# The four tiles of split weights put at four different places within 128 bytes of SBUF

## The chip, the cores and the metric

The kernel runs on one core of a Trainium2 chip. The metric is the device time of one launch in microseconds (us). The kernel before was timed in three runs: median 892.65 us, lowest 891.91, highest 894.43.

## The reference

Three parts follow each other. First an attention over 4 batches, 8 heads, 576 positions and 64 dimensions, mixed with a read of a memory matrix. Then two layers of experts over the 2304 rows of 512 numbers that the attention gives. Each layer picks one of 8 experts for a row and runs that expert's two products.

```python
local = np.matmul(softmax(mask(q @ k.T / 8)), v)
attn  = g * mem_out + (1 - g) * local        # -> x, 2304 rows of 512
# layer 1, layer 2 (same shape, other weights, other routing):
idx   = argmax(logits, axis=1)
for e in range(8):
    mask = idx == e
    h = np.maximum(x[mask] @ w1[e], 0.0)      # 512 -> 1024
    out[mask] = gate_w[mask, None] * (h @ w2[e])   # 1024 -> 512
```

## The kernel before, in words

The attention takes about the first 290 us. After it come two layers of steps. Each step takes 128 rows that go to one expert, gathers them, multiplies by `w1` (512 by 1024), applies the ReLU, multiplies by `w2` (1024 by 512) and writes 128 rows out.

The products are made in a 4-byte format (`F32R`) of less than full precision. To keep the precision, both operands are split into a high part and a low remainder, and each product is three matmuls: high rows by high weights, high rows by low weights, low rows by high weights (`mms`, L1235). One step has 48 such matmuls of 512 columns: 24 for `w1` (into `ph0` and `ph1`) and 24 for `w2` (into `py`). The rows are the stationary operand (128 by 128), the weights are the moving operand (512 columns, 2,048 bytes of each partition).

The split weights lie in four tiles. `Wh0` and `Wl0` are the high and low parts of `w1`, `Wh1` and `Wl1` those of `w2`. So in the trace `ph<-Wh` reads `Wh0`, `ph<-Wl` reads `Wl0`, `py<-Wh` reads `Wh1` and `py<-Wl` reads `Wl1`. Each tile has two halves of 16 KB of each partition: PE reads one half (`self.pv`) while the next expert's weights are split into the other (`self.wv`). Which half it is comes from a register, so the address of a matmul's weights is made by register instructions on PE's queue ahead of it. The order listings call them REGISTER_ALU (one operation) and ISA (several operations in one instruction); the trace calls them ALU_OP and FUSED_REGOPS.

A split of one eighth of an expert's weights (a chunk, 128 by 1024) is two instructions: ACT copies the staged chunk from `stg` to the high tile (`split_hi`, L898), DVE subtracts that from the staged chunk and writes the low tile (`split_lo`, L901). The chunks come in by DMAs that SP issues (`dma_chunks`).

The four tiles are taken one behind the other from a pool (`wp`, L1156 to L1158). In the built program of before they begin at bytes 69,344, 102,112, 134,880 and 167,648 of each partition. Each of these is 96 more than a multiple of 128, and since every matmul begins a multiple of 2,048 bytes into a half, every matmul's weights begin at 96 within 128 bytes too. The split rows (`b`, the stationary operand) also begin at 96; the rows of the second layer's first step (`x0`) begin at 32.

## Time and profile before

| what | us |
|---|---|
| median of three runs | 892.65 |
| lowest, highest | 891.91, 894.43 |
| the profiled execution, its own time | 894.2 |
| its span, first to last instruction | 892.4 |
| PE busy (matmuls) | 858.1 |
| DVE busy | 507.8 |
| ACT busy | 474.4 |

The profiled execution's time is 1.8 us more than its span. Matmuls are pipelined and the trace models their ends, so that one matmul's record reaches over the start of the next; what a matmul costs in a dense row of them is read from the distance between starts, not from its duration.

### The profile page before, as it was taken

To read this page: it belongs to the slowest core of one execution; us is meant where nothing else is said; L and a number is where in the kernel's file an instruction comes from. 1 tells how busy PE (TensorE), PEld (TensorE's weight loads), DVE (VectorE), ACT (ScalarE), POOL (GpSimd) and SP (SyncE) were. 2 spreads that over 40 slices of the span, in tenths; PEclk is the share of its full clock that TensorE was granted. 3 is DMA by queue.
4 is the path that set the end of the run, shared out by engine and by line. 5 is a ranking of instruction groups with operands and counts; after the bars stand their busy time and mean duration, and the time that the engine had idled before them with its cause. 6 is when DMAs were issued, how large, how long until landed. Compare 5 with 4: busy or idle time off the path is not lost. (4 is left out here: it accounts for less than half of the span.)

```text
span 892.4 us, 20618 instructions
## 1 busy us (share of the span) xinstructions
PE 858.1 (96%) x5187; PEld 675.0 (76%) x5187; DVE 507.8 (57%) x1589; ACT 474.4 (53%) x940; POOL 276.4 (31%) x375
## 2 busy tenths in 40 slices
PE   5999999999999999999999999999989999999996
PEld 2777677777668777877888877877868888888885
DVE  5657567568575866387536676644466414463520
ACT  3657657667566635376545545432366425564531
POOL 5457636536531111221221221211132112321221
PEclk9999999999999999999999999999999999999998
DMA  8424453423215266188424317022688415384111
GB/s 131 82 44 95 79 169 94 83 45 84 55 23 204 71 225 214 49 270 274 145 79 127 106 47 228 27 51 56 220 264 276 139 48 156 128 303 131 44 38 40
DMA packets 139813, 110.30 MB, mean 124 GB/s; under 512 B 107258, under 2 KB 107258, under 8 KB 139652
## 3 DMA queue, kind: packets, MB, share of 16 engines
q1 hardware_dynamic: 129252, 85.03, 33.3%
q0 software_dynamic: 8032, 23.22, 7.9%
q8 instruction: 53, 0.87, 0.4%
q14 instruction: 108, 0.88, 0.3%
q10 hardware_dynamic: 2368, 0.30, 0.2%
HBM read 90.32 MB, written 19.25 MB: 123 GB/s over the span
## 5 line engine op out<-in xcount | busy, mean ns | idle before, releaser
L1235 PE MATMUL py<-Wh,b 128*128 (+1 forms) x688 | 240.7, 406 | 2.5 <-DVE b L1179 2.4
L1235 PE MATMUL ph<-Wh,b 128*128 (+1 forms) x672 | 227.9, 400 | 0.7 <-ACTq L1246 0.7
L901 DVE TENSOR_TENSOR Wl<-stg,Wh 128x1024 f32 (+1 forms) x120 | 145.4, 1224 | 81.7 <-ACT Wh L898 71.7
L1235 PEld LDWEIGHTS py<-Wh,b 128*128 128x128 f32 x688 | 129.3, 188 | 32.5 <-issue 4.7
L1235 PEld LDWEIGHTS ph<-Wh,b 128*128 128x128 f32 x672 | 126.8, 189 | 27.1 <-ACTq L1246 1.1
L898 ACT ACTIVATE Wh<-stg 128x1024 f32 (+1 forms) x120 | 125.6, 1058 | 25.9 <-DVEq L1246 7.5
L1235 PE MATMUL py<-Wl,b 128*128 (+1 forms) x344 | 134.8, 392 | 0.0
L1235 PE MATMUL ph<-Wl,b 128*128 (+1 forms) x336 | 131.9, 392 | 2.1 <-DVEq L1246 2.0
L1179 DVE TENSOR_TENSOR b<-pt,b 128x512 fp32r<-128x512 f32 x86 | 59.4, 691 | 104.1 <-ACT b L1178 103.2
L263 ACT ACTIVATE att<-psat 128x512 f32<-128x512 f32 (+1 forms) x144 | 66.6, 463 | 78.2 <-PE psat L261 77.4
L284 PE MATMUL psav<-vb,att 128*128 128x128 f32 (+1 forms) x640 | 97.6, 283 | 0.9 <-ACT att L263 0.8
L284 PEld LDWEIGHTS psav<-vb,att 128*128 128x128 f32 x640 | 81.7, 192 | 20.9 <-ACT att L263 9.9
L1342 POOL DMA_INDIRECT out_dram<-ysb,xca x21 | 26.9, 1282 | 192.4 <-ACTq L1246 122.9
L1178 ACT ACTIVATE b<-pt 128x512 fp32r<-128x512 f32 x86 | 51.5, 598 | 62.9 <-PE pt L1347 61.7
L244 ACT ACTIVATE a<-a,mx 128x128 f32<-128x128 f32 (+3 forms) x128 | 71.0, 555 | 9.6 <-DVE mx L209 9.6
L1235 PEld LDWEIGHTS ph<-Wl,b 128*128 128x128 f32 x336 | 63.7, 190 | 14.8 <-DVEq L1246 2.7
L1235 PEld LDWEIGHTS py<-Wl,b 128*128 128x128 f32 x344 | 64.9, 189 | 9.8
L1337 ACT ACTIVATE ysb<-py,xca 128x512 f32<-128x512 f32 x42 | 28.8, 686 | 76.1 <-PE py L1235 65.4
L1144 POOL DMA_INDIRECT xg<-x_scratch,idx x48 | 55.9, 1165 | 40.5 <-POOL xca L1331 11.2
L209 DVE CUSTOM_DVE_ANT_0 a<-pss,wmask 128x128 f32<-128x128 f32 (+3 forms) x128 | 60.6, 478 | 9.0 <-PE pss L231 6.7
L1459 POOL DMA_DIRECT2D x_scratch<-xcb x21 | 11.9, 566 | 163.4 <-DVEq L1246 61.6
L261 PE MATMUL psat<-ident,a 128*128 128x128 f32 x320 | 58.2, 280 | 0.7 <-ACT a L244 0.6
(376 smaller groups left out, 1246.5 us busy)
## 6 DMA issues: line engine op xcount, KB each, us to landing
stg<-in_moe_w_dram SPq DMA_DIRECT2D x120, 512.0 KB, 4.9
x_scratch<-ysb POOLq DMA_DIRECT2D x22, 256.0 KB, 2.8
qkn<-in_q_dram SPq DMA_DIRECT2D x64, 72.0 KB, 2.5
qkn<-in_k_dram SPq DMA_DIRECT2D x60, 72.0 KB, 2.4
vb<-in_v_dram SPq DMA_DIRECT2D x32, 128.0 KB, 2.3
x_scratch<-xb SPq DMA_DIRECT2D x16, 256.0 KB, 3.3
x_scratch<-stg SPq DMA_DIRECT2D x11, 258.0 KB, 3.8
xg<-x_scratch,idx POOLq DMA_INDIRECT x48, 4.1
```

Of the source, the lines that this page charges most:

```text
L209: nc.vector.tensor_tensor_reduce(out=out, in0=ps, in1=mask, scale=-0.125, scalar=bound, op0=ALU.add, op1=ALU.min, accum_out=m)
L244: nc.scalar.activation(out=a[:, 0:N], in_=a[:, 0:N], func=AF.Exp, scale=-1.0, bias=mx, accum_out=rs_t[pi][:, c, j:j + 1])
L261: nc.tensor.transpose(ps[:, 128 * i:128 * i + 128], x, ident)
L263: nc.scalar.activation(out=att[:, 0:N], in_=ps[:, 0:N], func=AF.Copy)
L284: nc.tensor.matmul(av_t[pi][:, c, j:], att[:, 128 * kb:128 * kb + 128], vn[:, kb, j:, 0:D], start=(kb == 0), stop=(kb == c))
L898: return nc.scalar.activation(out=chunk(Wh, c, wv), in_=stg[:, c].unsqueeze(1), func=AF.Copy).ins
L901: return nc.vector.tensor_tensor(out=chunk(Wl, c, wv), in0=stg[:, c].unsqueeze(1), in1=chunk(Wh, c, wv).bitcast(F32), op=ALU.subtract).ins
L1144: return nc.gpsimd.indirect_dma_start(out=rows_of(t), out_offset=None, in_=rows, in_offset=bass.IndirectOffsetOnAxis(ap=idx[:, L, t:t + 1] ...
L1178: nc.scalar.activation(out=hi, in_=ps, func=AF.Copy)
L1179: nc.vector.tensor_tensor(out=lo, in0=ps, in1=hi.bitcast(F32), op=ALU.subtract)
L1235: mm = nc.tensor.matmul(ps, x[:, col:col + P], W, start=(first and q_ == qs[0]), stop=(last and q_ == qs[-1]))
L1337: nc.scalar.activation(out=ysb, in_=py, func=AF.Copy, scale=xc[:, 0:1])
```

## The change

The four tiles are still taken from the same pool in the same order. `Wh1` is made 4 elements (16 bytes) longer and used from its fifth element on, `Wl1` 16 elements (64 bytes) longer and used from its seventeenth on. The pool rounds the size of the longer `Wh1` up, so that `Wl0` and `Wl1` begin 32 bytes later as well.

```diff
     wp = ctx.enter_context(tc.tile_pool(name="wp", bufs=1, reuse_waits="tile"))
-    Wh.extend(wp.tile([P, 2, 4096], F32R, name=f"Wh{i}") for i in range(2))
-    Wl.extend(wp.tile([P, 2, 4096], F32R, name=f"Wl{i}") for i in range(2))
+    wt = lambda nm, o: wp.tile([P, 8192 + o], F32R, name=nm)[:, o:].rearrange("p (v n) -> p v n", v=2)
+    Wh.extend((wt("Wh0", 0), wt("Wh1", 4)))
+    Wl.extend((wt("Wl0", 0), wt("Wl1", 16)))
```

| tile | first byte used before | after | within 128: before | after |
|---|---|---|---|---|
| `Wh0` | 69,344 | 69,344 | 96 | 96 |
| `Wh1` | 102,112 | 102,128 | 96 | 112 |
| `Wl0` | 134,880 | 134,912 | 96 | 0 |
| `Wl1` | 167,648 | 167,744 | 96 | 64 |

No other tile moves. The number of instructions that compute or move data, their order on each engine and every semaphore wait are the same in both programs. What differs is how addresses are made. PE in one step of the first layer, at the start of the second product, before:

```order
L1235 ISA
L1235 MATMUL py<-Wh_3930,b_4031 128x512
L1235 REGISTER_ALU
L1235 MATMUL py<-Wl_3932,b_4031 128x512
L1235 MATMUL py<-Wh_3930,b_4032 128x512
L1347 MATMUL pt_3940<-ident,hs_4025 128x128 x4
```

The same place after (all lines behind the change stand one lower in the file):

```order
L1236 ISA
L1236 MATMUL py<-Wh_3930,b_4031 128x512
L1236 ISA
L1236 MATMUL py<-Wl_3932,b_4031 128x512
L1236 MATMUL py<-Wh_3930,b_4032 128x512
L1348 MATMUL pt_3940<-ident,hs_4025 128x128 x4
```

The one-operation instruction that made the address of `Wl1` from that of `Wh1` has become one with several operations. This is so at 160 places of the program, all of them on `Wl1`. DVE at the split of the first chunk of `w2`, before:

```order
L1246 COMPARE_AND_BRANCH
L901 ISA
L901 TENSOR_TENSOR Wl_3932<-stg,Wh_3930 128x1024
L1246 UNCONDITIONAL_BRANCH x2
L1262 UNCONDITIONAL_BRANCH
```

and after:

```order
L1247 COMPARE_AND_BRANCH
L901 ISA x2
L901 TENSOR_TENSOR Wl_3932<-stg,Wh_3930 128x1024
L1247 UNCONDITIONAL_BRANCH x2
L1263 UNCONDITIONAL_BRANCH
```

One more register instruction stands ahead of the split. This is so at 50 places; DVE's program has 757 of these instructions at this line in place of 707.

## Rows read from the trace of the kernel before

**Rows 1.** The page: busy time of the engines, TensorE's granted clock by slices.
```profile
PE 858.1 (96%) x5187; PEld 675.0 (76%) x5187; DVE 507.8 (57%) x1589; ACT 474.4 (53%) x940; POOL 276.4 (31%) x375
PEclk9999999999999999999999999999999999999998
```

**Rows 2.** The page's costliest groups: busy us, mean ns | idle before, releaser.
```profile
L1235 PE MATMUL py<-Wh,b 128*128 (+1 forms) x688 | 240.7, 406 | 2.5 <-DVE b L1179 2.4
L1235 PE MATMUL ph<-Wh,b 128*128 (+1 forms) x672 | 227.9, 400 | 0.7 <-ACTq L1246 0.7
...
L1235 PE MATMUL py<-Wl,b 128*128 (+1 forms) x344 | 134.8, 392 | 0.0
L1235 PE MATMUL ph<-Wl,b 128*128 (+1 forms) x336 | 131.9, 392 | 2.1 <-DVEq L1246 2.0 <-DVE Wl L901 0.2
```

**Rows 3.** The timeline, 502.0 to 505.5 us: start, duration, instruction.
```profile
502.03 0.39 PE L1235 MATMUL ph<-Wl,b 128*128 x1
...
502.26 0.62 PE L1235 MATMUL ph<-Wh,b 128*128 x2
...
502.65 2.15 ACT L898 ACTIVATE Wh<-stg 128x1024 f32 x2
502.71 0.39 PE L1235 MATMUL ph<-Wl,b 128*128 x1
...
503.73 2.54 DVE L901 TENSOR_TENSOR Wl<-stg,Wh 128x1024 f32 x2 [2.19 <-ACT Wh L898]
...
505.43 0.39 PE L1235 MATMUL ph<-Wl,b 128*128 x1
```

**Rows 4.** Windows: length, busy of PE, PEld, DVE, ACT, POOL, granted clock, DMA, GB/s.
```profile
501.81:505.43 3.62, 3.62 (x17) 3.00 (x16) 1.61 (x2) 3.32 (x5) 2.09 (x5) 1.00 0.16 57
600.60:603.20 2.60, 0.06 (x3) 0.00 (x0) 1.15 (x9) 0.69 (x1) 0.72 (x3) 1.00 0.03 7
604.20:606.90 2.70, 2.29 (x5) 1.72 (x6) 0.23 (x1) 0.00 (x0) 0.00 (x0) 0.50 0.30 100
300.00:892.40 592.40, 573.76 (x3037) 465.75 (x3036) 311.50 (x838) 284.50 (x420) 124.24 (x177) 0.99 0.43 139
```

**Rows 5.** The timeline of PE, 605 to 607 us.
```profile
605.20 1.05 PE L1235 MATMUL ph<-Wh,x 128*128 x2
606.05 0.63 PE L1235 MATMUL ph<-Wl,x 128*128 x1
606.48 0.63 PE L1235 MATMUL ph<-Wh,x 128*128 x1
606.91 0.41 PE L1288 MATMUL pm<-ident,ysb 128*128 128x128 f32 x1
```

**Rows 6.** The timeline of PE, 612.5 to 612.9 us.
```profile
612.54 0.39 PE L1235 MATMUL ph<-Wl,x 128*128 x1
612.76 0.40 PE L1235 MATMUL ph<-Wh,x 128*128 x1
```

**Rows 7.** Lines L1235, L901, L898: instructions, min/median/max ns, first and last start.
```profile
L1235 PEldq FUSED_REGOPS  x1647: 42/55/65, 344.6 to 882.2; - x183
...
L1235 PEldq ALU_OP  x128: 32/32/36, 544.4 to 882.4; - x128
...
L901 DVEq FUSED_REGOPS  x182: 53/93/118, 376.2 to 847.8; - x182
...
L901 DVE TENSOR_TENSOR Wl<-stg,Wh x120: 1215/1226/1261, 290.1 to 849.0; 128x1024 f32 x104, 128x1024 fp32r<-128x1024 f32 x16
...
L898 ACT ACTIVATE Wh<-stg x120: 1041/1061/1067, 287.7 to 847.0; 128x1024 f32 x104, 128x1024 fp32r<-128x1024 f32 x16
```

**Rows 8.** Waits: who for whom, us in total, times, longest.
```profile
PEld ph L1235 <- DVE Wl L901: 0.6, 1, 0.6
...
PEld ph L1235 <- ACT Wh L898: 0.3, 2, 0.2
...
PE ph L1235 <- DVE Wl L901: 0.2, 1, 0.2
```

## The prediction, made before the changed kernel was run

> **What bounds the kernel now.** I read the page's busy times first. PE is busy for 858.1 of 892.4 us and the next engine, DVE, for 507.8 [rows 1], so the time is PE's time. The groups of instructions say on what PE spends it after the attention: 2,040 matmuls of split weights stand in four groups, 688 on `Wh1`, 672 on `Wh0`, 344 on `Wl1` and 336 on `Wl0`, and they hardly wait for anyone: 2.5, 0.7, 0.0 and 2.1 us of idle time in all [rows 2]. Another 72 stand in smaller groups of the two layers' first steps and change nothing below.

> What one of them costs is read from the timeline, from start to start. From 502.03 to 505.43 us lie five groups of three matmuls, 15 in 3.40 us, which is 226.7 ns each [rows 3]. [...] At one column a cycle 512 columns would take 213.3 ns, so each matmul costs 13.3 ns more than that. This is the one number that a place in memory could touch directly, and 13.3 ns on 2,040 matmuls is 27.2 us, so it is worth a look at where it comes from.

> [...]

> **The change, part by part.**

> *Register instructions on PE.* The trace has 128 one-operation address instructions of 32 ns at this line beside 1,647 fused ones of 55 ns [rows 7]. The program turns 160 of its 320 into fused ones, so about 64 of the 128 that ran: 64 × (55 − 32) = 1.5 us on PE's queue, at most 128 × (65 − 32) = 4.2 us. They run ahead of the matmuls: three matmuls last 680 ns, two address instructions among them 110 ns. What hides them is the matmul before. I take 0; if that cover were gone it would be 1.5 us, up to 4.2.

> *Register instructions on DVE and ACT.* 182 fused instructions stood ahead of the 104 splits that ran with an address from a register [rows 7], so 78 had two and 26 had one. Half of the program's one-instruction splits get a second (50 of 101): 13 × 93 ns = 1.2 us. DVE is busy for 311.50 of 592.40 us from 300 us on [rows 4], and all that PE waits for a split is 0.6 + 0.3 + 0.2 = 1.1 us [rows 8]. I take 0. ACT's addresses are made by as many instructions as before.

> *Splits at another place.* ACT's copy takes 1,041 to 1,067 ns and DVE's subtraction 1,215 to 1,261 over all 120 [rows 7], whatever runs beside them, while both tiles and PE's reads lie at 96. There is no sign of a collision that another place could end. If the moved writes were dearer by the whole spread (46 ns on DVE, 120 times) that is 5.5 us on an engine with 281 us to spare in that stretch: 0 on the path. If they were cheaper, PE would gain at most the 1.1 us that it waits.

> *Reads at another place.* 688 + 344 + 336 = 1,368 matmuls read moved tiles, the 672 on `Wh0` don't. No row shows a weight tile of this format at any place but 96, so the price is bounded by the nearest numbers. Below: the whole 13.3 ns goes on all of them, 1,368 × 13.3 = 18.2 us. Above: the place costs the same 13.3 ns once more, 18.2 us. I take 0, for three reasons. The four groups have the same spacing, and the three that move do not differ from the one that stays (all at 96, so this alone is weak). The place of the other operand does not matter: with the stationary rows at 32 instead of 96 two starts are 612.54 and 612.76, again 0.22 to 0.23 us [rows 6]. And the spacing does not change while ACT and DVE write the other half of the same tiles: the copies run from 502.65 to 504.80 and the subtractions from 503.73 to 506.27, in the middle of the 15 even matmuls [rows 3].

> [...]

> *Sum.* 0 on PE's queue, 0 on DVE and ACT, 0 on the reads. The profiled execution has 894.2 us, 892.4 of them its span, and is 1.55 us above the median of the three runs, within their 891.91 to 894.43. With a sum of 0 the forecast is the median: 892.7 us.

> **The rivals.**

> *The low tile at 0 reads faster.* 2,048 bytes that begin at 96 touch 17 stretches of 128 bytes; at 0 they fill 16. 17/16 of 213.3 ns is 226.7, exactly the row. If PE is fed in such stretches, `Wl0` alone gets rid of the extra one (112 and 64 still touch 17): 336 × 13.3 = 4.5 us, 888.2. [...] Chance 0.09.

> *Reading and loading collide.* Weights and rows both begin at 96, and PE loads the next rows while it reads weights. If that equality costs the 13.3 ns, all three moved tiles lose it: 892.7 − 18.2 = 874.5. Against it stand the even starts with rows at 32 [rows 6]. Chance 0.08. Something smaller that is faster, such as half of the one or the other: 0.02.

> *`Wh1` at 112 reads slower.* 112 is the one place that is no multiple of 32. If a start off such a boundary costs one more hand-over of 13.3 ns, the largest group pays it: 688 × 13.3 = 9.2 us, 901.9. [...] Against it: nothing measured shows a price for 32. Chance 0.07.

> *The address instructions show.* If PE's queue is not ahead after a wait, their 1.5 to 4.2 us come out: about 895.5. Chance 0.04.

> **How the numbers follow.** No change at all has 0.70; its own range is 891 to 894.5, like the runs of before. Faster: 0.09 + 0.08 + 0.02 = 0.19. Slower: 0.07 + 0.04 = 0.11. Faster and slower mean by more than 0.3%, 2.7 us, about what a measurement of this kernel can tell from no change. The range reaches to the tile at 0 (888.2) and to the address instructions (895.5): 887.5 to 896.5 holds 0.70 + 0.09 + 0.04 = 0.83, and leaves out the two dear ends.

> **What the profile after would show.** Reads right: three matmuls in 0.68 us in `ph` and in `py`, and the groups' mean durations unchanged. The tile at 0 right: `ph<-Wl` to its next start 0.21 us, the others 0.23. A collision right: every pair that begins on `Wh1`, `Wl0` or `Wl1` 0.21 us. `Wh1` slower: 0.24 us after `py<-Wh` starts, nothing else changed. Splits right: 1,226 and 1,061 ns as before. Address instructions right: about 64 fewer of 32 ns and 64 more of 55 ns at the matmuls' line, about 13 more at DVE's, and no new idle time of PE that ends with "issue". The forecast is wrong if any of the four tiles has a spacing of its own.

## The result, and the profile after

The change made the kernel slower. Its median is 902.05 us (900.98 to 902.28) against 892.43 us (891.91 to 894.43) for the kernel before on the same chip: a ratio of 1.0101, interval 1.0084 to 1.0119. Measured a second time beside the experiments it was 900.70 us against 894.16, ratio 1.0072 (1.0056 to 1.0088). So the price is some 6 to 10 us. The forecast was 892.7 us with a range to 896.5, and it was wrong.

The page of the changed kernel, the rows that answer to [rows 1]:

```profile
PE 867.0 (96%) x5187; PEld 677.3 (75%) x5187; DVE 507.2 (56%) x1589; ACT 474.6 (53%) x940; POOL 276.8 (31%) x375
PEclk9999999999998999999999999998999999999999
```

PE is busy for 8.9 us more, the other engines for what they were. The span grew from 892.4 to 900.5 us. Its costliest groups, answering to [rows 2]:

```profile
L1236 PE MATMUL py<-Wh,b 128*128 (+1 forms) x688 | 242.0, 408 | 2.3 <-DVE b L1180 2.0 <-issue 0.2
L1236 PE MATMUL ph<-Wh,b 128*128 (+1 forms) x672 | 229.7, 402 | 0.6 <-ACTq L1247 0.6
...
L1236 PE MATMUL py<-Wl,b 128*128 (+1 forms) x344 | 135.7, 395 | 0.0
...
L1236 PE MATMUL ph<-Wl,b 128*128 (+1 forms) x336 | 133.9, 398 | 2.1 <-DVEq L1247 2.0
```

Nobody waits longer: the idle times are 2.3, 0.6, 0.0 and 2.1 us where they were 2.5, 0.7, 0.0 and 2.1. All four groups are a little longer, `ph<-Wh` too, though `Wh0` is the one tile that did not move. The timeline of PE shows what that is (start, duration, instruction; the stretch is like that of [rows 3]):

```profile
421.69 0.40 PE L1236 MATMUL ph<-Wl,b 128*128 x1
421.92 0.63 PE L1236 MATMUL ph<-Wh,b 128*128 x2
422.39 0.40 PE L1236 MATMUL ph<-Wl,b 128*128 x1
422.62 0.63 PE L1236 MATMUL ph<-Wh,b 128*128 x2
423.09 0.39 PE L1236 MATMUL ph<-Wl,b 128*128 x1
...
423.78 0.39 PE L1236 MATMUL ph<-Wl,b 128*128 x1
...
424.47 0.40 PE L1236 MATMUL ph<-Wl,b 128*128 x1
...
425.17 0.40 PE L1236 MATMUL ph<-Wl,b 128*128 x1
```

From 421.69 to 425.17 us lie 15 matmuls in 3.48 us, 232 ns each; [rows 3] had 15 in 3.40, 226.7 each. The steps of three are 0.70, 0.70, 0.69, 0.69, 0.70 where they were 0.68 every time. Over the whole trace, the mean distance between neighbouring starts of weight matmuls (of one line, from 300 us on, at the granted clock 1.00, under 260 ns apart) went from 228.2 ns (1,723 of them) to 231.8 (1,719). 1,719 × 3.54 = 6.1 us. This mean is called the spacing below. Sorted by the tile that the earlier of the two matmuls reads, it grew from 227.9 to 230.9 ns for `Wh0`, from 227.4 to 234.1 for `Wl0`, from 228.4 to 230.4 for `Wh1` and from 229.3 to 233.0 for `Wl1`.

The landmarks agree with that. First the line of the matmuls before, then after (min/median/max ns, first and last start):

```profile
L1235 PE MATMUL py<-Wh,b x688: 387/389/502, 313.1 to 884.6; 128*128 x160, 128*128 128x512 f32 x12
L1235 PE MATMUL ph<-Wh,b x672: 387/389/628, 305.5 to 878.2; 128*128 x156, 128*128 128x512 f32 x12
...
L1235 PE MATMUL ph<-Wh,x x16: 388/398/628, 603.2 to 612.8; 128*128 x16
```

```profile
L1236 PEldq FUSED_REGOPS  x1711: 46/55/60, 345.7 to 889.9; - x191
...
L1236 PE MATMUL py<-Wh,b x688: 387/396/503, 314.2 to 892.3; 128*128 x160, 128*128 128x512 f32 x12
...
L1236 PE MATMUL ph<-Wh,b x672: 387/393/632, 306.5 to 885.9; 128*128 x156, 128*128 128x512 f32 x12
...
L1236 PEldq ALU_OP  x64: 32/32/36, 546.8 to 884.2; - x64
...
L1236 PE MATMUL ph<-Wh,x x16: 387/488/787, 606.8 to 617.0; 128*128 x16
```

Up to the first `ph<-Wh,b` the changed kernel loses 1.0 us, 0.9 of it in the attention, which reads no moved tile (the first matmul of a product starts at 290.6 us instead of 289.7); in the first layer's steps 2.6 us (305.5 to 603.2, now 306.5 to 606.8); in the step on `x` 0.6; in the second layer's steps 3.5 (612.8 to 884.6, now 617.0 to 892.3); behind the last matmul 0.4. The 2.6 and 3.5 us are the 6.1 of the spacing. The 1.0 and the 0.6 us go with the granted clock, as the windows show, before and then after; the 0.4 us at the end are not explained here:

```profile
272.00:278.80 6.80, 6.80 (x53) 4.25 (x53) 5.15 (x20) 3.68 (x12) 2.80 (x3) 0.75 0.83 309
603.00:611.00 8.00, 6.89 (x31) 5.00 (x31) 0.53 (x2) 1.20 (x2) 1.61 (x3) 0.79 0.13 39
```

```profile
272.00:278.80 6.80, 6.80 (x38) 4.39 (x37) 4.49 (x18) 3.65 (x12) 2.79 (x3) 0.52 0.70 265
606.00:612.80 6.80, 5.82 (x15) 4.34 (x16) 0.23 (x1) 0.60 (x1) 0.73 (x2) 0.51 0.14 45
```

From 272.0 to 278.8 us the mean granted clock was 0.52 where it had been 0.75, and behind the break at 606 us 0.51 where it had been 0.79, so more of both stretches ran at the granted clock 0.50, which [rows 4] show from 604.20 to 606.90 us. This differs between executions: in the profile of the second measurement the step on `x` took 9.6 us as before, and the span was 897.5 us. It can be part of why the two ratios differ, though their intervals overlap, and it isn't what the experiments below are about.

### The profile page after: what moved, and what is told of

It reads as the page before. It is cut to its first block, busy times and chain, and to the rows that moved or that the text cites. A ratio compares the mean times of both kernels' runs of the same rounds, so it can differ in the third digit from the quotient of the medians.

```text
span 900.5 us, 20631 instructions
## 1 busy us (share of the span) xinstructions
PE 867.0 (96%) x5187; PEld 677.3 (75%) x5187; DVE 507.2 (56%) x1589; ACT 474.6 (53%) x940; POOL 276.8 (31%) x375
## 5 line engine op out<-in xcount | busy, mean ns | idle before, releaser
L901 DVE TENSOR_TENSOR Wl<-stg,Wh 128x1024 f32 (+1 forms) x120 | 145.4, 1224 | 84.9 <-ACT Wh L898 71.5
L898 ACT ACTIVATE Wh<-stg 128x1024 f32 (+1 forms) x120 | 125.6, 1057 | 26.3 <-DVEq L1247 7.8
L1236 PE MATMUL ph<-Wl,b 128*128 (+1 forms) x336 | 133.9, 398 | 2.1 <-DVEq L1247 2.0
```

What stands on the lines that cost most here:

```text
L898: return nc.scalar.activation(out=chunk(Wh, c, wv), in_=stg[:, c].unsqueeze(1), func=AF.Copy).ins
L901: return nc.vector.tensor_tensor(out=chunk(Wl, c, wv), in0=stg[:, c].unsqueeze(1), in1=chunk(Wh, c, wv).bitcast(F32), op=ALU.subtract).ins
L1236: mm = nc.tensor.matmul(ps, x[:, col:col + P], W, start=(first and q_ == qs[0]), stop=(last and q_ == qs[-1]))
```

## The experiments

The first reasons I could think of were the longer address instructions, a place within 128 bytes that is bad for a tile by itself, and neighbours at unlike places (PE reads `Wh` and `Wl` in turn). The spacing is worked out as above and decides more sharply than the time does. The first edit is shown against the change, the others against the kernel before, and statements are joined where the order of the tiles stays the same. The helper that makes a longer tile and uses it from a later element is that of the change:

```
wt = lambda nm, o=0: wp.tile([P, 8192 + o], F32R, name=nm)[:, o:].rearrange("p (v n) -> p v n", v=2)
```

**All four at 96 still, three of them moved by 128 or 256 bytes.**

```diff
-    Wh.extend((wt("Wh0", 0), wt("Wh1", 4)))
-    Wl.extend((wt("Wl0", 0), wt("Wl1", 16)))
+    Wh.extend((wt("Wh0"), wt("Wh1", 32)))
+    Wl.extend((wt("Wl0"), wt("Wl1", 32)))
```

> Wh1 and Wl1 are used 128 bytes later in tiles that much longer, so all four tiles stay at 96 within 128 bytes, while the addresses are made by the longer register instructions as in the change. Theory U (consecutive matmuls that read their weights at unequal places lose an even rhythm, 226.7 ns, and go at some 231 to 232): the places are equal, so 892 us and three matmuls in 0.68 us. Theory P (each place has its own price, 96 the cheapest of the four): 892. Theory D (weights must lie at the same place as the stationary rows, 96): 892. Theory A (the address instructions cost it): 900 to 902.

Measured: 898.79 us against 893.85, ratio 1.0054 (1.0041 to 1.0068). The spacing is 232.7 ns in `ph` and 229.2 in `py`. The timeline, 15 matmuls of `ph`:

```profile
420.27 0.39 PE L1238 MATMUL ph<-Wl,b 128*128 x1
...
423.76 0.40 PE L1238 MATMUL ph<-Wl,b 128*128 x1
```

That is 3.49 us. All tiles are at 96 within 128 here, so 128 bytes are not the period in which the place counts. Of the forecasts only that of the address instructions (900 to 902) is near. But PE's address instructions are as many of each kind as in the kernel before (1,647 fused and 128 plain; the edit made 13 more of them on DVE alone), and `ph` is slower all the same. So the longer ones on PE are not the cause.

**All four at 0 within 128.**

```diff
+    wp.tile([P, 8], F32R, name="gap")
+    Wh.extend((wt("Wh0"), wt("Wh1")))
+    Wl.extend((wt("Wl0"), wt("Wl1")))
```

> All four tiles at 0 within 128 bytes, the stationary rows still at 96. U: equal among themselves, 892 us, 226.7 ns. P: 0 is one of the dear places (ph<-Wl begins were 2 to 9 ns late in the changed kernel), so about 900 to 902. D: every matmul is now off the rows' place, 902 or more, some 231 to 232 ns. A: 892, the addresses are as in before.

Measured: 900.72 us, ratio 1.0073 (1.0053 to 1.0094), spacing 233.1 in `ph` and 232.8 in `py`. Equal neighbours, no tile at 112 and not one more address instruction on PE or DVE, and it is as slow as the change. Unlike neighbours and the address instructions are refuted as the cause, and so is the rival that 112 is the bad place.

**The tiles of `w1` unmoved, both tiles of `w2` at 112.**

```diff
+    Wh.append(wt("Wh0"))
+    Wl.append(wt("Wl0"))
+    Wh.append(wt("Wh1", 4))
+    Wl.append(wt("Wl1", 28))
```

> Wh0 and Wl0 at 96, Wh1 and Wl1 both at 112. U: neighbours in one product are equal, only the border between two products is not, so 892 to 894 us and 226.7 ns inside both products. P and D: the first product at 226.7, the second at about 231.4 as in the changed kernel, so half of the loss, 896 to 898. A: about 897.

Measured: 895.79 us, ratio 1.0022 (1.0011 to 1.0034). `ph` has its 227.8 ns back, `py` has 230.8. The timeline of `ph`:

```profile
418.00 0.39 PE L1238 MATMUL ph<-Wl,b 128*128 x1
...
421.40 0.39 PE L1238 MATMUL ph<-Wl,b 128*128 x1
```

15 matmuls in 3.40 us. A product that reads unmoved tiles alone is not slowed by the other one.

**The high tiles unmoved, the low ones 32 bytes up.**

```diff
+    Wh.extend((wt("Wh0"), wt("Wh1")))
+    wp.tile([P, 8], F32R, name="gap")
+    Wl.extend((wt("Wl0"), wt("Wl1")))
```

> Both high tiles at 96, both low tiles at 0, plain addresses. U: two of three neighbours in each product are unequal, no even rhythm, 900 to 902 us. P: only the low third of the matmuls is dearer, 895 to 896. D: the same, 895 to 896. A: 892.

Measured: 898.97 us, ratio 1.0056 (1.0038 to 1.0074), spacing 232.4 and 232.0. The time lies between the forecasts (895 to 896, or 900 to 902). In `ph` the spacing behind a matmul on `Wl0` went from 227.4 ns before to 234.6, and behind one on the unmoved `Wh0` from 227.9 to 231.0. So moving what one matmul in three reads slows the other two as well, which is what the unmoved `Wh0` showed in the change.

**The matmul by itself, at 41 sets of places.** What is left is a distance between the weights and something that did not move, and the nearest such thing is the other operand. So a kernel of its own leaves the computation out and runs rows of 42 matmuls of this kind, all on the value 0.5, with nothing beside them (shortened):

```
for t in range(14):                      # c, w: the next 128 and 512 columns
    for x, y in ((BHI + bh, WHI + hi), (BHI + bh, WLO + lo), (BLO + bl, WHI + hi)):
        nc.tensor.matmul(o, big[:, x + c:x + c + 128], big[:, y + w:y + w + 512], ...)
```

> Leaves the whole computation out: 41 rows of 42 matmuls of 512 columns in the kernel's pattern (high rows by high weights, high rows by low weights, low rows by high weights), each row with other places of the two weight regions (moving operand) and the two row regions (stationary operand), nothing else running. Theory D2 (what counts is the distance of the weights from the rows, over a stretch longer than 128 bytes, since e1 moved by 128 and lost the rhythm): 226.7 ns a matmul where both distances are 0 or -256 bytes, also when weights and rows are shifted together, some 229 to 233 at most other distances. Theory U2 (unequal neighbours among the weights alone): 226.7 wherever high and low weights are equal, whatever the rows' place. Theory P (price of a place): the shift of weights and rows together changes it. Theory E (other engines or DMAs beside it are needed for the loss): 226.7 everywhere.

Distances below are weights minus rows, in bytes. The timeline draws such matmuls together; a row of n has n − 1 spacings and the last one's 0.39 us. Six of them, in order: distance 0; 64; 256; weights and rows both moved by 64; the change's `ph` (0 and 32); its `py` (16 and 96):

```profile
34.77 7.42 PE L47 MATMUL ps<-big 128*128 128x512 f32 x32
...
72.73 7.63 PE L47 MATMUL ps<-big 128*128 128x512 f32 x32
...
151.84 7.42 PE L47 MATMUL ps<-big 128*128 128x512 f32 x32
...
285.73 7.65 PE L47 MATMUL ps<-big 128*128 128x512 f32 x33
...
362.68 7.57 PE L47 MATMUL ps<-big 128*128 128x512 f32 x32
...
372.64 7.33 PE L47 MATMUL ps<-big 128*128 128x512 f32 x31
```

That makes 7.03/31 = 226.8 ns, 233.5, 226.8, 226.9, 231.6 and 231.3. In the mean of the last 24 spacings of each set, from one execution:

| distance of weights from rows, bytes | ns |
|---|---|
| 0, ±256, 512, 768, 1024 | 226.67 |
| 16; 32, 48, 64; 80; 96; 112 | 231.7; 233.3; 231.1; 233.3; 231.1 |
| 128; 160; 192, 224, 384 | 232.1; 234.3; 233.3 |
| weights and rows moved together by 32, 64, 128, 256, 512 | 226.67 |
| low weights alone by 16, 32, 64, 128 | 232.1, 231.7, 231.9, 233.3 |
| low weights alone by 256, 512, 1024 | 226.67 |
| low rows alone by 32, 128; by 256, 512 | 233.3, 231.1; 226.67 |

Moving both operands together changes nothing, so it is the distance that counts, and a distance of whole 256 bytes is as good as 0: 226.67 ns. The distances of the table that aren't cost 4.4 to 7.6 ns in the mean of the row. Two sets with one of the weight tiles at a good distance and the other 128 off it cost only 2.2 (high and low at −256 and −128, at −128 and 0: 228.9). The first of them is, within 256 bytes, the set of the table with the low weights alone off by 128, which has 233.3: off the good distance the distance alone does not fix the spacing. Nothing but PE works here (from 48 to 57 us DVE, ACT and POOL are busy for 0.00 us), so no other engine has a part in it.

With that the kernel of before can be read again: its weights begin at 224 within 256 bytes and its rows `b` too, a distance of 0 for all four tiles. The change made it 0 and 32 for `ph`, 16 and 96 for `py`.

**The weights as in the second experiment, and the rows moved after them.**

```diff
+    wp.tile([P, 8], F32R, name="gap")
...
     bufs = Bufs(lambda i: fp.tile([P, 512], F32R, name=f"b{i}") if i < 6 else hs_[i - 6])
+    fp.tile([P, 56], F32, name="gap2")
```

The first gap puts the weights 32 bytes up. The rows' pool lies against the other end of the memory, so the second gap, 224 bytes behind its last tile, puts all its rows 224 lower, which is 32 higher within 256.

> All weight tiles at 0 within 128 bytes as in e2, and the split rows put at 0 as well (their pool ends 224 bytes earlier), so the distance of weights and rows is again a multiple of 256 bytes. Theory D2 (the distance of weights from rows within 256 bytes): the rhythm of 226.7 ns is back and with it 892 to 894 us. Theory P (0 is a dearer place than 96): stays at 900 to 901 as in e2.

Measured: 894.18 us against 894.04, ratio 1.0012 (0.9994 to 1.0029), spacing 227.7 and 228.5. Twelve matmuls of `py` take 2.72 us, 226.7 each:

```profile
427.40 0.39 PE L1239 MATMUL py<-Wl,b 128*128 x1
...
430.12 0.39 PE L1239 MATMUL py<-Wl,b 128*128 x1
```

The weights lie where they cost 0.7% in the second experiment, and the cost is gone because the rows followed.

**The rows alone, the weights untouched.**

```diff
     bufs = Bufs(lambda i: fp.tile([P, 512], F32R, name=f"b{i}") if i < 6 else hs_[i - 6])
+    fp.tile([P, 8], F32, name="gap2")
```

All rows of the pool lie 32 bytes lower.

> The weights stay where they were, only the rows (and what else is in their pool) move down by 32 bytes. D2: the rhythm is lost as in e2, 232 to 233 ns, 899 to 901 us, with no weight tile moved. P and U2 (only the weights' places count): 892 to 894.

Measured: 899.58 us, ratio 1.0067 (1.0044 to 1.0089), spacing 233.1 and 232.9. 15 matmuls of `ph`:

```profile
504.16 0.40 PE L1235 MATMUL ph<-Wl,b 128*128 x1
...
507.67 0.39 PE L1235 MATMUL ph<-Wl,b 128*128 x1
```

3.51 us. Not one weight tile moved, and the whole loss is there.

**Three tiles moved by 256 bytes, with the change's longer address instructions, and without them.**

```diff
+    Wh.extend((wt("Wh0"), wt("Wh1", 64)))    # first kernel
+    Wl.extend((wt("Wl0"), wt("Wl1")))
```

```diff
+    Wh.append(wt("Wh0"))                     # second kernel
+    wp.tile([P, 64], F32R, name="gap")
+    Wh.append(wt("Wh1"))
+    Wl.extend((wt("Wl0"), wt("Wl1")))
```

> Wh1, Wl0 and Wl1 are used 256 bytes later (Wh1 by an offset in its tile, so that its addresses are made as in the change). D2: 256 is no shift, 226.7 ns, 892 to 894 us, against 898.8 of e1, which moved the same tiles by 128 and 256. A period longer than 256 bytes, or the address instructions: 897 to 901.

> The same three tiles 256 bytes later as in e7, but by an empty gap in the pool, so that addresses are made as before. If the 1.9 us that e7 was over the kernel before came from the longer address instructions, this one is at 1.000 of before; if they came from the place (a longer period than 256 bytes), it is at 1.002 like e7. Spacing 226.7 ns in either case.

Measured: the first 896.10 us against 894.04, ratio 1.0021 (1.0006 to 1.0035), spacing 228.3; the second 894.81 against 894.16, ratio 1.0004 (0.9989 to 1.0018), spacing 228.2. Both keep the rhythm. In the second, 15 matmuls of `ph`:

```profile
502.94 0.39 PE L1239 MATMUL ph<-Wl,b 128*128 x1
...
506.34 0.39 PE L1239 MATMUL ph<-Wl,b 128*128 x1
```

3.40 us again. Between the two stand the address instructions (PE has 1,711 fused and 64 plain ones in the first, as in the change, and 1,647 and 128 in the second, as before). They ran on two chips, so each goes by its own kernel before: 2.1 and 0.7 us above it. The intervals overlap, and whether these instructions cost anything stays open.

**Finer places, shorter matmuls, other formats.** A second kernel of the matmul by itself. One idea for the mechanism was that the reading of weights and the loading of the next rows take turns in SBUF, so that fewer loaded columns would cost less.

> Leaves the whole computation out: rows of 42 matmuls as in m1, with fine distances of weights from rows, other lengths of the moving operand (512, 384, 320, 256 columns) and of the stationary one (128, 64, 32 columns), mixed distances, and two other number formats. Theory D2 with a collision of the two reads (the next stationary operand is read while the weights stream): distances that are no multiple of 256 cost the same 5 to 7 ns a matmul whatever the moving length, as long as the load fits beside it, and about half and a quarter with 64 and 32 stationary columns; 2-byte and full 4-byte formats, which stream fewer bytes a cycle, show less or nothing. Theory S (a start that misses its turn, nothing to do with the load): the cost is independent of the stationary operand's columns. No distance under 226.7 ns is expected by the first scan; one would make a faster kernel.

| set | ns at distance 0, 64, 128 |
|---|---|
| 512 columns, 128 columns of rows loaded | 226.7, 228.9, 232.1 |
| 512 columns, 64 columns of rows loaded | 230.0, 228.3, 229.4 |
| 512 columns, 32 columns of rows loaded | 231.7, 231.7, 231.0 |
| 384 columns | 173.3, 173.3, 176.1 |
| 320 columns | 146.7, 146.7, 146.7 |
| 256 columns | 120.0, 117.8, 118.6 |
| bf16, 512 columns | 215.8, 215.8, 215.8 |
| full fp32, 512 columns, each of its two passes | 429.2, 429.2, 429.2 |

Thirteen distances from 4 to 252 bytes that are no multiple of 16 gave 228.6 to 240.0, with 240.0 at 20, 68, 100 and 132; 16 sets with high and low operands at unlike places gave 230.8 to 237.8. Not one of the 512-column sets in `F32R` came under 226.67. The two passes of full fp32 are read from the trace, which has 252 records of the kernel's 126 such matmuls. Of the weights, a partition's 2,048 bytes took 226.7 ns in `F32R` and 2 × 429.2 in full fp32, the 1,024 of bf16 took 215.8. Fewer loaded columns did not cost less, so that idea found no support; with 64 or 32 of them distance 0 itself was no longer fast (230.0 and 231.7). Distance 64 gave 228.9 here and 233.3 in the first scan, so off the good distance the spacing can settle at more than one value; that it depends on how the row started is likely, but not shown.

**The change once more.**

> The change itself once more, beside e8 and e9 on one chip. Distances of weights from rows within 256 bytes: 0 (Wh0), 16 (Wh1), 32 (Wl0), 96 (Wl1). All theories: 900 to 902 us, spacing 231 to 232 ns in both products.

Measured: 900.70 us, ratio 1.0072 (1.0056 to 1.0088), spacing 231.8, as the first time.

**All other rows at the good distance too**, to see whether it gains anything:

```diff
-    xgt.extend(fp.tile([P, XR], F32, name=f"xg{i}") for i in range(2))
+    xgt.extend(fp.tile([P, 576], F32, name=f"xg{i}")[:, 0:XR] for i in range(2))
```

> The weights as before; the gather buffers are made longer so that everything in the rows' pool (x0, hs, xg, ysb, b) begins a multiple of 256 bytes from the weights; before, x0, hs and the first gather buffer were 64 and the second 32 bytes off. If a start after a break (transposes of hs and xg) falls into the rhythm sooner, the 229 to 233 ns of the first eight matmuls shrink: up to 1.59 ns x 1,747 = 2.8 us, 0.997 of before. If the break itself upsets it, 1.000.

Measured: 894.62 us, ratio 1.0002 (0.9987 to 1.0016), spacing 227.9. The `x` rows, which stood off the good distance in the kernel before, are brought to it here, and nothing is gained that the time shows. No version found beats the kernel before.

The scan by itself and the kernel's own spacing, side by side:

| kernel | distances within 256 (high, low), `ph`; `py` | by itself | in the kernel |
|---|---|---|---|
| before | 0, 0; 0, 0 | 226.7; 226.7 | 227.7; 228.7 |
| the change | 0, 32; 16, 96 | 231.7; 231.1 | 232.1; 231.4 |
| first experiment | 0, 128; 128, 0 | 233.3 or 228.9; 228.9 | 232.7; 229.2 |
| all at 0 | 32, 32; 32, 32 | 233.3; 233.3 | 233.1; 232.8 |
| second pair at 112 | 0, 0; 16, 144 | 226.7; 231.1 | 227.8; 230.8 |
| low tiles by 32 | 0, 32; 0, 32 | 231.7; 231.7 | 232.4; 232.0 |
| rows alone by −32 | 32, 32; 32, 32 | 233.3; 233.3 | 233.1; 232.9 |

In the kernel a good row shows 1 to 2 ns more than by itself, since each break (transposes between the products) is followed by some matmuls at 228 to 233 ns before the rhythm is back (in the trace of before the mean of the first eight spacings behind a break is 228.4 to 233.3 ns by their place, and of the tenth to sixteenth 226.6 to 226.8).

## Why the prediction was wrong

**The failed step is "Reads at another place": "I take 0".** That term came out at 6.1 us (1,719 × 3.54 ns), because the change took the weights from a distance of 0 from the rows to 32, 16 and 96 bytes. The 0 stood on three reasons, and two could not carry it.

- "The place of the other operand does not matter", from the two starts of [rows 6]. The runs show the opposite: the loss comes and goes with the weights' distance from the other operand. The neighbouring rows of before already read otherwise:

```profile
609.84 0.39 PE L1235 MATMUL ph<-Wl,x 128*128 x1
610.07 0.63 PE L1235 MATMUL ph<-Wh,x 128*128 x2
610.54 0.39 PE L1235 MATMUL ph<-Wl,x 128*128 x1
610.77 0.39 PE L1235 MATMUL ph<-Wh,x 128*128 x1
```

 Four spacings in 0.93 us, 232 ns. But this stretch is short and begins behind a break, where `b` rows show the same, so it could settle nothing in either direction: with the `x` rows brought to the good distance, in the last experiment, the same four take 0.93 us again. One spacing of 0.22 us was taken for a rhythm.
- "The four groups have the same spacing": they had, because all four stood at distance 0. I had called this reason weak, and it was: the kernel before held no other case.
- "The spacing does not change while ACT and DVE write": true, and the scan confirms that other engines have no part in it. It excluded a cause that was none.

The bounds of ±18.2 us for this term held the result; the value in them and its count did not. The term counted the 1,368 matmuls on moved tiles alone. The price is not confined to them: the spacing behind the unmoved `Wh0` grew by 3.0 ns, which makes 1.6 of the 6.1 us. The sign that it named, "any of the four tiles has a spacing of its own", did come: 234.1 and 233.0 ns behind the low tiles, 230.9 and 230.4 behind the high ones.

The 13.3 ns of those bounds are what 226.7 has above 213.3, and the prediction names no row for the 213.3. The second scan shows them: at distance 0 a matmul took 120.0 ns with 256 columns and 226.7 with 512, so 0.4167 ns a column and 213.3 for 512. At the granted clock 0.50 [rows 4] a matmul of 512 columns took 427 ns [rows 5], twice 213.5.

**The rivals.** *`Wh1` at 112* gave 901.9 us, within the measured runs, by a mechanism that is refuted: `ph`, which never reads `Wh1`, is slower, and the kernel without any tile at 112 is as slow. *Reading and loading collide at equal places* had the right pair of operands and the sign reversed: equal places are the good case. *The low tile at 0 reads faster*: with all tiles at 0 the spacing is 233 ns, and with the rows moved after them it is back at the 228 of before, not lower. *The address instructions show*: they are not the loss; whether 1.5 us of them come out is open. None of the four had the mechanism, so it is luck that one of them names the measured time.

**What held.** PE is the bound and what a matmul costs is read from starts. The register instructions came out as counted: 1,647 + 64 = 1,711 fused, 128 − 64 = 64 plain, and 13 more at DVE's line, and the four groups of PE waited no longer. The splits kept their durations:

```profile
L901 DVEq FUSED_REGOPS  x195: 53/93/118, 377.1 to 855.0; - x195
...
L901 DVE TENSOR_TENSOR Wl<-stg,Wh x120: 1212/1226/1246, 291.1 to 856.2; 128x1024 f32 x104, 128x1024 fp32r<-128x1024 f32 x16
```

```profile
L898 ACT ACTIVATE Wh<-stg x120: 1040/1060/1067, 288.6 to 854.2; 128x1024 f32 x104, 128x1024 fp32r<-128x1024 f32 x16
```

1,226 and 1,060 ns, where [rows 7] has 1,226 and 1,061.

**What stays open:** the mechanism itself, so why the period is 256 bytes and why off it one distance has more than one spacing; why even at distance 0 there are 13.3 ns above the 213.3 of the columns, and the 0.2% of the first of the two kernels moved by 256.

## What to carry to other kernels

Where a kernel is bound by `F32R` matmuls, look at where both operands lie: here weights and rows a multiple of 256 bytes apart kept a matmul of 512 columns, with 128 columns of rows loaded, at 226.7 ns, and every other distance tried cost 2 to 13 ns. A tile that is made a few bytes longer moves everything behind it in its pool, so an edit that seems to touch one tile can break this for all. And a rhythm is read from a long unbroken run of starts, a dozen or more; before a place is priced at nothing, ask whether the kernel holds a second case at all.
